# A four-byte touch read ahead of the gate weights: 32 runs instead of 64

## The chip, the cores and the metric

The kernel runs on one core of a Trainium2 chip. The metric is the device time of one execution in microseconds (us), taken over several executions. All executions are fast (no lowered clock, and none over 1.5% above the fastest of its kernel). The profile's span (first to last instruction) is 1.7 to 1.8 us shorter than the device time. The engines are PE (matmul), PEld (its weight load), DVE (vector), ACT (scalar), POOL, and SP, which issues most of the DMAs; ACT issues a few DMAs too.

## The reference

A layer norm of x (2048 x 512) feeds two branches whose outputs are added to x: a state-space layer (a complex linear recurrence over 2048 steps) and a gated feed-forward layer.

```python
xn = layernorm(x)
g = silu(xn @ w_gate)          # w_gate: 512 x 1376
u = xn @ w_up                  # w_up:   512 x 1376
out = x + S5(xn) + (g * u) @ w_down
```

The contraction of 512 is cut into four K tiles of 128 rows.

## The kernel before

The order of the instructions on each engine is computed at build time by a list scheduler from estimated durations; a DMA's estimate contains its byte count. The kernel begins with a start-up in which the first four tiles of x (128 tokens each) are loaded one by one, normalized, transposed on PE, and multiplied with the gate weights as soon as each is there. The loads of this start-up are issued from two queues, SP and ACT, in this order in the code:

```python
x_load(0)                                    # SP, 128 KB
x_load(1)                                    # SP
act_q = [dma("ld_touch", tch[0:16], wg_v[0:128:8, :, 0:2], [("tch",)], 16 * 16, eng="act")]
act_q.append(wg_load("a0", 0, 2, eng="act", order=(act_q[-1],)))   # gate K tiles 0 and 1, 448 KB
x_load(2)                                    # SP
act_q.append(wg_load("a1", 2, 3, eng="act", order=(act_q[-1],)))   # gate K tile 2, 224 KB
wg_load("a2", 3, 4)                          # SP, gate K tile 3
x_load(3)                                    # SP
```

The touch copies two bf16 numbers (4 bytes) from every eighth row of each K tile of the gate weights into a small tile `tch`. No instruction reads `tch`. ACT must issue the touch before it issues the gate load `a0`.

PE fills the time until the first tile is normalized with warm-up matmuls on constants:

```python
pe_warm(9, 512, wbank)
pe_warm(2, 128, wbank)
ln_chunk0()                                  # statistics and normalization of x tiles 0..3 (DVE, ACT)
xt_tile_fine(0, 0, wbank)                    # transposes on PE, evacuated by ACT
# ... (cut) ...
# gate matmuls of one x tile, K tile by K tile: wait for the gate load of that K tile
g.add("pe", mm, reads=[("wg", "a%d" % max(k - 1, 0)) for k in range(k0, k1)] + [("xnTq", q, k) for k in range(k0, k1)], ...)
```

## Time and profile before

The first timing of the kernel was 179.23 us (median of 3).

| What | Value | Where it is read |
|---|---|---|
| PE busy | 173.5 of 177.5 us | page, busy times |
| chain of waits | 96% PE | page, chain |
| x tile 0 landed | 3.10 us | chain |
| first gate matmul | 5.83 us | timeline of PE |
| gate K tiles 0-1 landed | 5.03 us | landings in the trace |

The busy line of the page (busy us, share of the span, instructions; a few matmul records can be missing from a trace):

```profile
PE 173.5 (98%) x935; PEld 83.7 (47%) x935; DVE 162.7 (92%) x284; ACT 88.0 (50%) x116; POOL 11.7 (7%) x22
```

The chain of work that ended last, first 8 us (columns: start us, us, what):

```profile
0.79 2.31 DMA x_sb<-in_A_x_dram
3.10 0.02 issue
3.12 0.71 DVE st L530
...
4.92 0.61 ACT xn_sb L548
5.53 0.05 issue
5.58 0.28 PE pb L582 x2
5.86 0.11 PE pb L477
5.97 1.02 PE pb L803 x18
```

All waits of PE in the whole execution (who waited for whom: us in total, times, longest):

```profile
PE pb L477 <- PEq L1076: 0.8, 1, 0.8
PE pb L582 <- DVE xn_sb L517: 0.6, 1, 0.6
PE pb L582 <- ACT xn_sb L548: 0.2, 1, 0.2
```

The chain begins with a DMA, the load of x tile 0, goes through the normalization on DVE and ACT, and from 5.58 us on it is PE until the last output. And PE waits for nothing after that.

### The profile page before, as it was taken

The page shows a single profiled execution, that of the slowest core. Times are in us where ns is not written, and L with a number is a line of the kernel's source. Part 1 is how long each engine was busy: PE and PEld are TensorE (multiplying, and loading weights), DVE is VectorE, ACT ScalarE, POOL GpSimd, SP SyncE. Part 2 cuts the span into 40 slices and gives each one's busy share as a digit, 9 for nine tenths or more (in the row PEclk, how much of TensorE's full clock was granted, in tenths as well). Part 3 has the DMA queues.
Part 4 walks back from the last instruction along what each step waited for, and adds up shares of the span by engine and source line. Part 5 has one row for each costly group of instructions (what it writes and reads, how often), then busy time and mean ns, then how long its engine had stood idle before and what let it go on. Part 6 is the DMA issues. An engine that isn't in the chain of part 4 may idle for free.

```text
span 177.5 us, 2429 instructions
## 1 busy us (share of the span) xinstructions
PE 173.5 (98%) x935; PEld 83.7 (47%) x935; DVE 162.7 (92%) x284; ACT 88.0 (50%) x116; POOL 11.7 (7%) x22
## 2 busy tenths in 40 slices
PE   7899999999999999999999999999999999999994
PEld 3794444444444444444444444444444444444743
DVE  2966999699999999999999999999999999999933
ACT  4679989679999655026565560000965520000000
POOL 3023300040000000260000000000000000000000
PEclk9999999999999999999999999999999999999999
DMA  5994562664946000001520000001000000001022
GB/s 168 311 365 112 118 131 53 170 145 107 352 100 48 0 0 0 0 30 63 110 39 0 0 0 4 0 30 59 30 0 4 0 0 0 0 0 51 11 89 89
DMA packets 23014, 12.37 MB, mean 70 GB/s; under 512 B 15228, under 2 KB 23004, under 8 KB 23004
## 3 DMA queue, kind: packets, MB, share of 16 engines
q1 hardware_dynamic: 22508, 11.54, 24.7%
q10 hardware_dynamic: 496, 0.69, 1.2%
q8 instruction: 7, 0.11, 0.2%
q14 instruction: 3, 0.02, 0.0%
HBM read 6.46 MB, written 2.10 MB: 48 GB/s over the span
## 4 chain that ended last, share of the span: by engine, by line
PE 96%; DMA 1%; DVE 1%; ACT 1%; issue 0%
PE pb L759 36%; PE pb L959 21%; PE pb L972 16%; PE pb L876 16%; PE pb L803 4%; PE pb L839 2%; DMA x_sb<-in_A_x_dram 1%; PE pb L849 1%; PE pb L582 1%; DVE st L530 0%; ACT xn_sb L548 0%; ACT nm L545 0%; ACT sd L524 0%; DVE x_sb L977 0%; DVE mv L522 0%
## 5 line engine op out<-in xcount | busy, mean ns | idle before, releaser
L916 DVE TENSOR_TENSOR_SCAN rot<-sm,car,rot 128x512 bf16<-128x512 f32 x32 | 38.9, 1266 | 0.1
L959 PE MATMUL pb<-wd,hT 128*128 128x512 bf16 (+3 forms) x198 | 38.8, 355 | 0.0
L759 PE MATMUL pb<-xnT,wu 128*128 128x512 bf16 x160 | 37.3, 379 | 0.0
L759 PE MATMUL pb<-xnT,wg 128*128 128x512 bf16 x132 | 31.3, 379 | 0.0
L972 PE MATMUL pb<-W,hss 128*128 128x512 bf16 (+2 forms) x144 | 28.3, 355 | 0.0
L876 PE MATMUL pb<-xnT,BT 128*128 128x512 bf16 x128 | 28.1, 379 | 0.0
L959 PEld LDWEIGHTS pb<-wd,hT 128*128 128x128 bf16 (+1 forms) x198 | 18.5, 98 | 19.9
L759 PEld LDWEIGHTS pb<-xnT,wu 128*128 128x128 bf16 x160 | 15.6, 98 | 18.9 <-issue 0.2
L829 ACT ACTIVATE uf<-pb 128x1024 bf16<-128x1024 f32 x20 | 20.6, 1028 | 7.3 <-PE pb L759 6.1
L771 ACT ACTIVATE sg<-pb 128x1024 bf16<-128x1024 f32 x20 | 20.2, 1025 | 8.0 <-PE pb L759 7.1
L972 PEld LDWEIGHTS pb<-W,hss 128*128 128x128 bf16 x144 | 13.4, 98 | 14.3
L759 PEld LDWEIGHTS pb<-xnT,wg 128*128 128x128 bf16 x132 | 12.7, 98 | 15.7 <-ACT xn_sb L506 0.4
L876 PEld LDWEIGHTS pb<-xnT,BT 128*128 128x128 bf16 x128 | 12.5, 98 | 15.1
L883 ACT ACTIVATE u_sb<-pb 128x1024 bf16<-128x1024 f32 x16 | 16.2, 1019 | 5.7 <-PE pb L876 5.4
L977 DVE TENSOR_TENSOR x_sb<-pb,x_sb 128x512 bf16<-128x512 f32 (+2 forms) x18 | 11.0, 622 | 3.5 <-PE pb L972 3.4
L831 DVE TENSOR_TENSOR hT<-sg,uf 128x1024 bf16<-128x1024 bf16 x20 | 13.4, 681 | 0.0
L506 ACT ACTIVATE xn_sb<-x_sb,nmr,rstd 128x512 bf16<-128x512 bf16 x8 | 6.0, 803 | 9.6 <-DVE nmr L503 9.6
L858 ACT ACTIVATE sg<-pb 96x1024 bf16<-96x1024 f32 x2 | 2.0, 1014 | 17.1 <-PE pb L839 17.1
L482 DVE BATCH_NORM_STATS2 st<-x_sb 128x6 f32<-128x512 bf16 x12 | 7.4, 682 | 3.2 <-DMA x_sb<-in_A_x_dram 3.2
L907 DVE TENSOR_TENSOR rot<-rot,cosT 128x2048 bf16<-128x2048 bf16 x8 | 9.7, 1218 | 0.1
L907 DVE TENSOR_TENSOR rot<-rot,sin 128x2048 bf16<-128x2048 bf16 x8 | 9.8, 1219 | 0.0
L907 DVE TENSOR_TENSOR rot<-u_sb,cosT 128x2048 bf16<-128x2048 bf16 x8 | 9.7, 1218 | 0.0
(81 smaller groups left out, 145.6 us busy)
## 6 DMA issues: line engine op xcount, KB each, us to landing
out_dram<-x_sb SPq DMA_DIRECT2D x15, 128.0 KB, 1.7
x_sb<-in_A_x_dram SPq DMA_DIRECT2D x3, 512.0 KB, 7.4
wd<-in_B_w_down_dram SPq DMA_DIRECT2D x1, 1280.0 KB, 6.9
wu<-in_B_w_up_dram SPq DMA_DIRECT2D x1, 768.0 KB, 5.3
wu<-in_B_w_up_dram SPq DMA_DIRECT2D x1, 608.0 KB, 7.4
x_sb<-in_A_x_dram SPq DMA_DIRECT2D x4, 128.0 KB, 3.6
wg<-in_B_w_gate_dram SPq DMA_DIRECT2D x1, 480.0 KB, 6.2
wg<-in_B_w_gate_dram ACTq DMA_DIRECT2D x1, 448.0 KB, 3.8
```

The costliest lines, as they stand in the source:

```text
L482: return g.add("dve", lambda e, a=a: e.bn_stats(out=st[:, a, :], in_=x_sb[:, a, :]), reads=[("x", a)], writes=[("st", a)], name="bnst%d" % ...
L759: inst = e.matmul(pbank[0:fs, bk, :].rearrange("p (j t) -> p j t", j=4), lhsT=w[:, kt, i * 128:i * 128 + fs], rhs=xnT[:, c % 2, :, kt, :], ...
L771: g.add("act", lambda e: e.activation(out=sg[rows, sl, 0:n, :].rearrange("p a t -> p (a t)"), in_=pair_f32(rows, bk, 512 * n), func=AF.Sil ...
L829: g.add("act", lambda e: e.activation(out=uf[rows, ul, 0:n, :].rearrange("p a t -> p (a t)"), in_=pair_f32(rows, bk, 512 * n), func=AF.Ide ...
L831: g.add("dve", lambda e: e.tensor_tensor(out=hT[rows, hb, i0:i0 + n, :], in0=sg[rows, sl, 0:n, :], in1=uf[rows, ul, 0:n, :], op=ALU.mult), ...
L876: inst = e.matmul(pbank[:, bk, :].rearrange("p (j t) -> p j t", j=4), lhsT=BT[:, ri, kt, pt * 128:(pt + 1) * 128], rhs=xnT[:, c % 2, :, kt ...
L883: g.add("act", lambda e: e.activation(out=u_sb[:, us].rearrange("p r t -> p (r t)"), in_=pair_f32(slice(0, 128), b0), func=AF.Identity), r ...
L907: tt = lambda out, a, b, op, r, w, nm: g.add("dve", lambda e: e.tensor_tensor(out=out, in0=a, in1=b, op=op), reads=r, writes=w, name="%s_% ...
L916: g.add("dve", lambda e, A0=A0, A1=A1, k=k, ri=ri, pt=pt: e.tensor_tensor_scan(out=A1[:, k, ri, :], data0=rr[:, pt:pt + 1].to_broadcast([1 ...
L959: inst = e.matmul(pbank[:, bk, 0:nc_], lhsT=hT[0:fs, hb, i, lt * 128:(lt + 1) * 128], rhs=wd[0:fs, i, c0:c0 + nc_], start=(i == 0), stop=F ...
L972: inst = e.matmul(pbank[:, bk, 0:nc_], lhsT=hss[:, hb, pt, ri, lt * 128:(lt + 1) * 128], rhs=W12[:, ri, pt, c0:c0 + nc_], start=False, sto ...
L977: g.add("dve", lambda e, bk=bk, a=a, c0=c0, nc_=nc_: e.tensor_tensor(out=x_sb[:, a, c0:c0 + nc_], in0=pbank[:, bk, 0:nc_], in1=x_sb[:, a, ...
```

## The change

The touch was presumably there to reach into the gate weights before the large loads do. The change lets it cover two of the four K tiles, with half as many descriptors. The large loads and everything after them are untouched.

```diff
-        act_q = [dma("ld_touch", tch[0:16], wg_v[0:128:8, :, 0:2], [("tch",)], 16 * 16, eng="act")]
+        act_q = [dma("ld_touch", tch[0:16, 0:2], wg_v[0:128:8, 0:2, 0:2], [("tch",)], 16 * 8, eng="act")]
```

## The prediction

> **What bounds the kernel.** The share table has PE busy 98% of the 177.5 us span (173.5 us). The chain of waits is PE 96%: from the first gate matmul at 5.8 us to 175.2 us it is PE work. PE's waits sum to 1.6 us, all before 5.8 us, none on a weight load. So only the landing of x tile 0 (the chain begins with that DMA, 0.79 to 3.10 us, then DVE and ACT until 5.53 us) or a new gap in PE's stream can move the time.
>
> **What the change does.** The touch read is the first DMA on the ACT queue. Nothing reads its tile or waits for it. It is 64 runs of 4 bytes (16 partitions x 4 K tiles) and becomes 32. The DMA packet records show 4-byte packets of the ACT queue from 1.95 to 2.55 us: 80 of them, 9 ns each. The Trainium skill (DMA: Bandwidth & Descriptors, "Why a DMA increments its semaphore by 16 and not by 1") says that one descriptor moves one contiguous run and that each of 16 engines ends with a semaphore write; 64 + 16 fits. After it I expect 48, or 3 instead of 5 per engine: 18 ns of each engine saved.
>
> **What moves.** The gate load of K tiles 0-1 follows on the same ring: issued at 1.23, first packet at 2.59 us. x tile 0 needed 1.03 us from issue to first packet, so the load could start at about 2.3 to 2.4 us; half of the hold-up, 0.05 to 0.15 us, may be gained. x tile 2 (first packet about 4.0 us, when that load ends) may move as much.
>
> **On the critical path.** Nearly nothing: gate tiles 0-1 at 5.03 us, first used at 5.83 (0.8 slack); tile 2 at 6.09, used at about 6.63 (0.5); tile 3 at 6.59, used at about 7.2 (0.6). x tile 2 lands at 5.91 and DVE reads it at 5.93, but the transposes that this feeds find PE busy. The slack would also cover 0.2 to 0.4 us of slower starts of the two untouched K tiles. Exposed is only x tile 0: its reads end by about 2.53 us, just before the gate load starts. If that load starts 0.1 us earlier, its 1792-byte packets (74 ns and more) meet the tail of x tile 0 or its writes: +0.0 to +0.1 us. Fewer touch packets: -0.02 us.
>
> **Predicted time: 179.2 us**, 8 in 10 between 179.0 and 179.5. Chances: faster by over 2% 0.005, within 2% 0.985, slower by over 2% 0.01.
>
> **What would show it.** 48 packets of 4 bytes on the ACT queue before the first gate load; first 1792-byte packet at about 2.5 us; landing of x tile 0 within 0.1 us of 3.10; first gate matmul within 0.15 us of 5.83; PE waits still without a weight DMA; PE busy within 0.3 us of 173.5.
>
> **What would make it wrong.** (1) The instruction order is computed from estimates that contain the byte count of the touch (256 to 128 bytes, about 1 ns in the model); a near tie could flip an order and cost or save up to 1 us. (2) The touch does more than I think for K tiles 2 and 3, and their loads land over 0.5 us later: PE would wait at about 6.6 or 7.2 us. (3) x tile 0 is delayed by the earlier gate load by more than 0.2 us.

## More of the kernel before

The DMA queue of ACT (packets, MB, share of 16 engines' span) and the touch itself (KB, us from issue to landing):

```profile
q10 hardware_dynamic: 496, 0.69, 1.2%
tch<-in_B_w_gate_dram ACTq DMA_DIRECT2D x1, 0.2 KB, 2.1
```

## The result, and the profile after

The changed kernel took 179.53 us (median of 6, 179.08 to 179.96), the kernel before in the same comparison 179.26 us (179.17 to 179.78). The ratio is 1.0005 with a 95% interval of 0.9983 to 1.0028. (A ratio is the mean time of one kernel's fast runs over that of the other's of the same rounds, so it is not quite the ratio of the medians.) The computed instruction order of every engine is the same as before, apart from the touch.

The same lines of the changed kernel: busy times, then the first part of the chain, then the waits of PE, then the queue of ACT and the touch.

```profile
PE 173.4 (98%) x927; PEld 83.8 (47%) x935; DVE 162.7 (92%) x284; ACT 87.7 (49%) x116; POOL 11.7 (7%) x22
```

```profile
0.79 2.26 DMA x_sb<-in_A_x_dram
...
4.87 0.61 ACT xn_sb L548
5.48 0.05 issue
5.53 0.29 PE pb L582 x2
5.81 0.11 PE pb L477
5.92 1.02 PE pb L803 x18
```

```profile
PE pb L477 <- PEq L1076: 0.8, 1, 0.8
PE pb L582 <- DVE xn_sb L517: 0.2, 1, 0.2
PE pb L582 <- ACT xn_sb L548: 0.2, 1, 0.2
```

```profile
q10 hardware_dynamic: 464, 0.69, 1.1%
tch<-in_B_w_gate_dram ACTq DMA_DIRECT2D x1, 0.1 KB, 2.1
```

The queue of ACT carries 496 - 464 = 32 packets less, exactly the 32 runs taken away. x tile 0 landed 0.05 us earlier (0.79 + 2.26 = 3.05 us), and the gate matmuls began 0.05 us earlier. Nothing else of note happened in this execution. What is left to explain is why nothing happened, what the touch is good for, and where a scatter of 0.9 us comes from.

### The profile page after: what moved, and what is told of

Its sections match the earlier page's. It is cut to its first block, busy times and chain, and to the rows that moved or that the text cites. A ratio compares the mean times of both kernels' runs of the same rounds, so it can differ in the third digit from the quotient of the medians.

```text
span 177.4 us, 2421 instructions
## 1 busy us (share of the span) xinstructions
PE 173.4 (98%) x927; PEld 83.8 (47%) x935; DVE 162.7 (92%) x284; ACT 87.7 (49%) x116; POOL 11.7 (7%) x22
## 4 chain that ended last, share of the span: by engine, by line
PE 95%; DMA 1%; DVE 1%; ACT 1%; issue 0%
PE pb L759 36%; PE pb L959 21%; PE pb L876 16%; PE pb L972 15%; PE pb L803 4%; PE pb L839 2%; DMA x_sb<-in_A_x_dram 1%; PE pb L849 1%; PE pb L582 1%; DVE st L530 0%; ACT xn_sb L548 0%; ACT nm L545 0%; ACT sd L524 0%; DVE x_sb L977 0%; DVE mv L522 0%
## 5 line engine op out<-in xcount | busy, mean ns | idle before, releaser
L959 PE MATMUL pb<-wd,hT 128*128 128x512 bf16 (+3 forms) x194 | 38.1, 355 | 0.2
L759 PE MATMUL pb<-xnT,wu 128*128 128x512 bf16 x160 | 37.3, 379 | 0.0
L759 PE MATMUL pb<-xnT,wg 128*128 128x512 bf16 x132 | 31.3, 380 | 0.0
L759 PEld LDWEIGHTS pb<-xnT,wu 128*128 128x128 bf16 x160 | 15.7, 98 | 18.9 <-issue 0.2
L759 PEld LDWEIGHTS pb<-xnT,wg 128*128 128x128 bf16 x132 | 12.7, 98 | 15.7 <-issue 0.4
```

What stands on the lines that cost most here:

```text
L759: inst = e.matmul(pbank[0:fs, bk, :].rearrange("p (j t) -> p j t", j=4), lhsT=w[:, kt, i * 128:i * 128 + fs], rhs=xnT[:, c % 2, :, kt, :], ...
L959: inst = e.matmul(pbank[:, bk, 0:nc_], lhsT=hT[0:fs, hb, i, lt * 128:(lt + 1) * 128], rhs=wd[0:fs, i, c0:c0 + nc_], start=(i == 0), stop=F ...
```

## The experiments

All were timed with five rounds against the kernel before on the same chip. The first four shared one chip, the next four a second one and the last three a third one. The order of all other instructions was kept as in the changed kernel, except in the last experiment. All results were correct. The edits are shown shortened and against the changed kernel, that of e11 against e2. Two theories stood at the start:

- **Inert**: neither the number of runs nor what they touch matters.
- **Warming**: the touch makes the first real reads of the gate weights quicker, so the half left out is missed.

A third: **spacer**. ACT needs about 0.4 us to issue the touch; that alone keeps the large gate load out of the way while x tile 0 is read.

This table is worked out from the traces of all executions that were profiled, one per kernel and run. A landing is the last of the completion updates of a DMA. "Gate" is the first gate matmul, "full" the first full-width matmul (512 columns) after the start-up (L759), "tail" the time from the start of that to the end of the last DVE add.

```
run           touch runs   x0    x1    K0-1    K2    x2    K3    gate   full   tail
before        64           3.10  4.35  5.03   6.09  5.91  6.59  5.83   12.94  162.57
after         32           3.05  4.07  5.21   6.16  5.81  6.77  5.78   12.86  162.56
e1 (after)    32           2.92  4.77  6.26   6.97  6.60  7.54  6.30   13.64  162.56
e2            none         3.31  4.96  4.63   5.64  5.96  6.56  6.06   13.14  162.57
e3            32, w_up     2.91  3.99  4.97   5.98  5.34  6.55  5.64   12.71  162.57
e4            512          3.07  3.90  5.77   6.75  6.15  6.95  5.82   13.19  162.56
e5            1            2.83  4.38  5.21   6.12  5.55  6.72  5.71   12.92  162.57
e6 (after)    32           3.02  4.00  4.92   6.17  5.49  6.77  5.75   12.83  162.56
e7            32 + 32      3.00  3.46  5.95   7.17  5.29  6.81  6.01   13.46  162.56
e8            32 + 32 + 32 3.72  4.42  5.55   7.29  6.42  7.50  6.45   13.65  162.56
e9            none (swap)  3.84  3.65  5.49   6.17  4.16  6.75  6.72   15.44  162.56
e10           32           2.93  3.98  4.29/5.26  7.24  5.04  7.05  5.98   13.52  162.73
e11           none         3.41  5.00  4.65   5.66  6.00  6.58  6.16   13.24  162.56
```

The last column decides where to look. From the first full-width matmul to the end, twelve of thirteen executions took the same 162.56 or 162.57 us. (In e10 a further 0.17 us went at about 25 us, at the start of the state-space matmuls.) So nearly every difference between these kernels, and between two executions of one kernel, arises in the first 13 us.

### The changed kernel again (e1 and e6)

No edit.

> The changed kernel once more, five rounds, to tell a true difference from the scatter of the first timing (179.08 to 179.96 us). Inert theory (the number of touch runs does not matter): ratio to before within 0.9985 to 1.0015, first packet of the first gate load again near 2.6 us and x tile 0 landing within 0.1 us of 3.1. Rival (the second half of the touch was worth something): ratio 1.001 to 1.002 and clear of 1, with the loads of K tiles 2 and 3 landing later than 6.09 and 6.59 us again.

> The changed kernel a third time. Eleven timings of it so far scatter from 179.08 to 179.98 us, and the profile of its slowest one shows PE waiting 0.3 us for the first gate load, of which one of 16 parts landed 0.85 us after the others. If the change makes such late parts likelier: at least two of five timings above 179.6 us, and the mean 0.1 to 0.25 us above that of before. If it was luck: mean within 0.1 us of before.

e1: ratio 1.0013 (0.9997 to 1.0029), timings 179.12 to 179.98 us. e6: ratio 0.9989 (0.9973 to 1.0005), 179.12 to 179.76 us. In the second comparison it was the kernel before that scattered up to 180.00 us. Together with the first result, 18 timings of the changed kernel have a mean of 179.45 us and the 28 of the kernel before in those comparisons 179.41 us; the difference, 0.04 us, is below its standard error of 0.09 us. The hint of a loss in e1 was by this luck of that comparison. Neither expectation fitted to the letter: in e1 x tile 0 landed at 2.92 us, further from 3.1 us than the 0.1 us that the inert theory allowed, and the mean of e6 lies 0.22 us below that of the kernel before, not within 0.1 us.

The profiled execution of e1 happened to be its slowest, 179.98 us. Its waits of PE, then its chain up to the first gate matmuls:

```profile
PE pb L477 <- PEq L1076: 0.8, 1, 0.8
PE pb L803 <- DMA wg<-in_B_w_gate_dram: 0.3, 1, 0.3
```

```profile
0.79 0.41 ACTq L402
1.20 0.03 issue
1.23 5.03 DMA wg<-in_B_w_gate_dram
6.26 0.04 issue
6.30 1.29 PE pb L803 x18
```

Here the chain begins on ACT's DMA queue and not with x tile 0: x tile 0 landed early (2.92 us), but the gate load of K tiles 0-1 landed at 6.26 us. Of its 16 completion updates, 14 came by 4.96, the fifteenth at 5.41 and the last at 6.26 us: one of sixteen parts was 0.85 us late, and each of the next four loads (K2, x2, K3 and x tile 3) again had a last completion 0.7 us behind its last but one. The slack of 0.8 us that a typical trace shows is real, but a late part uses it up. Why that part was late the trace does not tell. Whether the other slow timings have the same cause was not seen, as only one execution of each run is profiled. A second, smaller source shows in the traces of e1 and e5: the first three gate matmuls start 83 to 107 ns apart and the next ones 55 to 57 ns, which costs about 0.13 us.

### No touch (e2)

```diff
-        act_q = [dma("ld_touch", ...)]
-        act_q.append(wg_load("a0", 0, 2, eng="act", order=(act_q[-1],)))
+        act_q = []
+        act_q.append(wg_load("a0", 0, 2, eng="act")); act_q[0].est += 330.14; act_q[0].nbytes += 54450
```

The last two additions change only the estimates, so that the computed order stays as it was.

> No touch at all; the order of all other instructions is kept (the estimate of the first gate load is raised by what the touch had). Inert theory: time within 0.1 us of before. Spacer theory (the touch matters only because its issue holds the gate load back by 0.4 us, so that x tile 0 reads alone): the first gate packet at 1.9 to 2.2 us instead of 2.6, x tile 0 lands 0.15 to 0.5 us later than 3.1 and the time rises by the same 0.15 to 0.5 us. Warming theory (the touch makes the first reads of the gate weights quicker): first gate packets take longer than now and the first gate load needs clearly more time from its first packet to landing (2.4 us now).

Median 179.55 us (179.45 to 179.73), ratio 1.0012 (1.0000 to 1.0024). The whole of its range lies above the median of the kernel before, 179.25 us. The start of its chain:

```profile
0.79 2.52 DMA x_sb<-in_A_x_dram
3.31 0.02 issue
3.34 0.70 DVE st L530
```

x tile 0 landed at 3.31 us, the gate matmuls began at 6.06 instead of 5.83 us, and the time rose by 0.3 us. So the touch is not inert as a whole: without it the kernel is slower, as the spacer theory expected (this interval alone just reaches 1.0000; e11 repeats it). One of its numbers missed: the gate load was expected to start at 1.9 to 2.2 us and started at 2.65 us. Against the warming theory, the gate load took 1.98 us from its first packet to landing, not more than the 2.43 us of the kernel before. The DMA packet records tell more (counted from the trace: reads of x on SP's queue that had begun by 2.4 us, the last of the 16 completion packets that end x tile 0, the first packet of the first gate load, and the packets of both that began between 3.0 and 3.7 us; in e9, described below, ACT's queue carries x tiles 1 and 2 and has 43 and 124 reads more in the two columns):

```
run      x reads by 2.4   last completion packet of x0   first gate packet   3.0-3.7: x reads   gate packets
before   113              2.60                           2.59                13                  98
after    104              2.65                           2.61                49                  93
e2        44              2.97                           2.65                 0                 150
e11       58              3.05                           2.55                 2                 151
e9        17              3.31                           2.95                13                  71
```

Without the touch, x tile 0 and the gate load are issued at the same moment (0.79 us). The reads of x tile 0 then go at less than half the pace although the gate load's own packets do not begin before 2.65 us. The trace shows where the pace is lost: 12 of the 128 packets of x tile 0 took 406 to 675 ns (in e11 10 of them took 404 to 601 ns), all begun by 2.25 us, where a usual one takes 46 ns; with a touch none of the 128 took over 361 ns in any trace. And x tile 1, issued at 1.25 us, has no packet at all between 3.0 and 3.7 us while the gate load runs: it lands at 4.96 instead of 4.35 us, behind the gate load. In this stretch what was issued first was served first, across the two queues. (If the DMA engines took whole loads from the two queues in turn, it would look the same: both give the order x0, K0-1, x1, K2, x2 that is seen here, and no run tells the two apart.)

### The touch on another tensor (e3)

```diff
-wg_v[0:128:8, 0:2, 0:2]
+wu_v[0:128:8, 0:2, 0:2]
```

> The same 32-run touch, but of the up weights, which the first gate loads do not read. Spacer theory and inert theory: the same time as the changed kernel within 0.1 us, gate loads landing as in it (5.2, 6.2, 6.8 us, each within 0.2). Warming theory: as without a touch, gate landings later by 0.2 us or more.

Median 179.27 us (179.03 to 179.48), ratio 0.9999 (0.9986 to 1.0012). A touch of the up weights, which the first gate loads do not read, does everything that the touch of the gate weights does, and the gate loads land as early (4.97, 5.98, 6.55 us; 0.22 to 0.25 us before the 5.2, 6.2 and 6.8 us expected, a little more than the 0.2 us allowed, but earlier and not later). The reverse can be read too: the up weights were touched here, yet among the first 64 packets of their large load at about 6.3 us, 12 took over 200 ns and the slowest 953 ns, where they had 19 and 674 ns in the kernel before, in which nothing had touched them. The warming theory falls.

### Eight times the runs (e4)

```diff
-tch = sb("tch", [16, KT, 2], B16)
+tch = sb("tch", [128, KT, 2], B16)
-        act_q = [dma("ld_touch", tch[0:16, 0:2], wg_v[0:128:8, 0:2, 0:2], ...
+        act_q = [dma("ld_touch", tch[:], wg_v[:, :, 0:2], ...
```

> The touch eight times the original (128 partitions x 4 K tiles, 512 runs of 4 bytes, 33 packets per engine). If a run costs only its 9 ns of engine time: the first gate load begins 0.2 to 0.3 us later, lands by 5.4 us, before its first use at 5.83; x tile 0 unchanged within 0.1 us; time within 0.15 us of before. If a run costs what the original touch took in sum (0.6 us for 5 packets per engine, 0.12 us each): the first gate load begins about 3 us later, PE waits for it for over 1 us, and the time rises by over 1 us.

Median 179.75 us (179.50 to 179.89), ratio 1.0021 (1.0009 to 1.0033). The first branch of the expectation came nearer: the first gate packet came at 2.90 us, 0.3 us later than with 64 runs (2.59 us), about what 9 ns times 28 more packets per engine gives (0.25 us); x tile 0 was in time (3.07 us). The match may be partly chance: the touch's own packets began later (2.36 instead of 1.95 us) and took no longer from first to last (0.53 against 0.61 us). Its landing and its verdict on the time were wrong, though. The gate loads landed at 5.77 (not by 5.4) and 6.75 us, and in the chain PE stops for K tile 2:

```profile
5.94 0.83 PE pb L803 x14
6.77 0.11 issue
6.88 0.38 PE pb L803 x4
```

After 14 matmuls (two K tiles of seven) PE needs K tile 2, which landed at 6.75 us. The slack behind the gate loads is therefore small: this kernel is 0.4 us slower (means: 179.70 against 179.31 us for the kernel before; the profiled execution, 179.53 us, shows 0.25 us of it at the first full-width matmul). From 64 to 32 runs the same arithmetic gives 2 packets per engine, or 18 ns, which no comparison here can see.

### One run of four bytes (e5)

```diff
-tch[0:16, 0:2], wg_v[0:128:8, 0:2, 0:2]
+tch[0:1, 0:1], wg_v[0:1, 0:1, 0:2]
```

> A touch of a single run of 4 bytes: the issue on ACT stays (0.4 us), the descriptors go from 32 to 1. Spacer theory (only the place of the first gate load in the order of issue counts, behind x tile 1): first gate packet at 2.45 to 2.65 us as with 32 and 64 runs, x tile 1 lands by 4.4 us, before the gate load is done, time 179.2 to 179.4 us. Descriptor theory (the runs themselves hold the gate load back): as without a touch, first x reads slow, x tile 1 landing near 4.9 us, time 179.5 us or more.

Median 179.21 us (179.15 to 179.48), ratio 0.9986 (0.9972 to 1.0000). The queue of ACT confirms that next to nothing of the touch is left (464 - 418 = 46 packets less than the changed kernel: 31 runs and 15 completions):

```profile
q10 hardware_dynamic: 418, 0.69, 1.1%
```

x tile 0 landed at 2.83 us and the time was as good as with 32 or 64 runs. The issue of the touch on ACT suffices; its data do not matter. The first gate packet, at 2.73 us, was slightly later than expected; the issue of this touch took 0.52 instead of 0.41 us, so the gate load was issued at 1.34 instead of 1.23 us.

### Two touches (e7), and everything later (e8)

```diff
 act_q = [dma("ld_touch", tch[0:16, 0:2], ...)]
+act_q.append(dma("ld_touch2", tch[0:16, 2:4], wg_v[0:128:8, 2:4, 0:2], ..., eng="act"))    # e7 and e8
+dma("ld_touch3", tch[0:16, 4:6], wg_v[0:128:8, 2:4, 0:2], ...)                             # e8 only: SP, ahead of x_load(0)
```

(In e8 `tch` is made twice as wide. The estimates of the added DMAs are set to 0, so that the order of the rest stays.)

> The original 64 runs in two DMAs of 32 on ACT, so that the first gate load is issued 0.4 us later (1.65 instead of 1.23 us) and comes behind x tile 2 in the order of issue. Spacer theory: x tile 1 and x tile 2 land earlier (x tile 2 by about 5.2 instead of 5.9 us), the first gate load later by 0.3 to 0.5 us (5.3 to 5.5 us, first use at 5.8), the time within 0.2 us of before or up to 0.4 us longer when a late part of it passes 5.8 us. Inert theory: all landings as before.

> One more touch of 32 runs ahead of x tile 0 on SP and one more on ACT, so that all first loads are issued 0.4 us later in the same order. If the chain begins with x tile 0 and nothing after it has slack, as the prediction says: x tile 0 lands near 3.5 us and the time rises by 0.35 to 0.45 us, ratio 1.002 to 1.0025. If there is slack behind x tile 0: less than 0.2 us.

e7: median 179.65 us, ratio 1.0005 (0.9991 to 1.0020) against a kernel before that scattered widely; its mean, 179.61 us, is 0.32 us above that of e6 on the same chip (179.28 us). As expected x tiles 1 and 2 landed earlier (3.46 and 5.29 us) and the gate loads later (5.95 and 7.17 us), later even than the 0.3 to 0.5 us foreseen. PE waited for K tile 2:

```profile
PE pb L803 <- DMA wg<-in_B_w_gate_dram: 0.3, 1, 0.3
```

There is a second cost that had not been foreseen: ACT issues DMAs and computes. Its table load begins after the last issue. It began at 2.23 us before and at 2.70 us in e7, and the square root that the normalization needs came at 4.20 us although x tile 0 was earlier (3.00 us). Timeline of ACT in e7 (start us, us, what):

```profile
1.71 0.96 ACTq L402 DMA_DIRECT2D wg<-in_B_w_gate_dram  x2
2.70 1.28 ACT L466 ACT_TABLE_LOAD   x1 [2.70 <-issue]
4.00 0.29 ACT L466 ACTIVATE sm<-epst 128x1 f32<-128x1 f32 x1
4.20 0.28 ACT L524 ACTIVATE sd<-mv,epst 128x1 f32<-128x1 f32 x1
```

Before, the same two activations stood at 3.52 and 4.07 us with a wait of 0.25 us between them. One spacer fits in front of the table load, a second does not. In this trace that cost is hidden, as the chain runs through K tile 2 (landed at 7.17 us).

e8: median 179.82 us, ratio 1.0021 (1.0007 to 1.0035), as expected for a delay of 0.4 us that passes to the end. In its profile x tile 0 was issued at 1.25 us and landed at 3.72 us, later than the 3.5 us expected:

```profile
0.79 0.39 SPq L402
1.18 0.07 issue
1.25 2.47 DMA x_sb<-in_A_x_dram
3.72 0.02 issue
```

Compared with the profiled execution of e6, x tile 0 came 0.70 us later, the gate matmuls 0.70 us later (6.45 against 5.75 us) and the full-width matmuls 0.82 us later. There is no slack behind x tile 0.

### Another spacer (e9)

After the order has been computed, x tiles 1 and 2 are moved to ACT, the gate loads to SP behind x tile 0, and the touch is dropped:

```diff
+for e_, ns in (("act", ["ld_x1", "ld_x2"]), ("sp", ["ld_x0", "ld_wga0", "ld_wga1", "ld_wga2"])):
+    streams[e_] = [dl[n] for n in ns] + [t for t in streams[e_] if t.name not in early]
```

> No touch, but the same order of issue as with it: x tiles 1 and 2 go out on ACT, x tile 0 and the gate loads on SP, so that the first gate load is the second DMA of SP (issued at about 1.2 us) behind x tile 0 and x tile 1; the order of every other instruction is kept. Spacer theory: any DMA that holds the first gate load in its place does what the touch does: gate loads and x tiles 1 and 2 land within 0.25 us of their places in the changed kernel, time within 0.15 us of it. Rival (x tile 0 lands late whenever a large load is issued at the same moment, 0.79 us, as the run without a touch suggests): x tile 0 at 3.2 us or later and the time 0.15 to 0.35 us longer. If the touch does something of its own: also longer, with x tile 0 in time.

Median 179.80 us (179.60 to 181.78), ratio 1.0022 (1.0008 to 1.0036). The rival was right about x tile 0: x tile 0 and x tile 1, both issued at 0.79 us, landed together at 3.84 and 3.65 us, and by 2.4 us only 17 reads of x tile 0 had begun. (By the ratio the time rose by 0.39 us, a little more than the 0.35 us it allowed.) The chain:

```profile
0.79 3.05 DMA x_sb<-in_A_x_dram
3.84 0.02 issue
3.86 0.70 DVE st L530
```

So the late landing in e2 was no peculiarity of the gate weights: another large load issued at the same moment, x tile 1, goes with a late x tile 0 too. The three kernels with a late x tile 0 (e2, e9, e11) are, however, also the three without a touch, and no run has a touch and another large load both issued at 0.79 us; that the touch itself does something is thus not excluded by them. x tile 1 speaks against it: in the kernels with a touch it is issued within 0.1 us of the first gate load and lands 2.65 to 3.52 us after its issue, but in e7, where the second touch is issued beside it in place of the gate load, 2.21 us after. The order of issue was not kept as intended either, as x tile 2 (1.21 us) came ahead of the gate load (1.25 us) and landed at 4.16 us. The profiled execution, 181.78 us, had bad luck on top, which the other five timings (up to 180.04 us) do not show: PE waited 0.7 us before the first transposes and ran the first gate matmuls at half the pace. Timeline of PE (start us, us, what), e9:

```profile
6.72 2.13 PE L803 MATMUL pb<-xnT,wg 128*128 128x128 bf16 x18
```

The same 18 matmuls took 1.16 us in the changed kernel. From the first of them to the transposes behind them it is 1.92 us in e9 and 1.00 us in the changed kernel, or 107 and 56 ns for each. The Trainium skill ("TensorE: Matmul & The Clock Gate", section "What you observe") gives these very two gaps, 107 and 56 ns, for a PE before and after its warm-up. The trace agrees: its record of the clock grants PE the full clock only from 10.23 us on, where the kernel before had it from 3.52 us.

### The first gate load in two (e10)

```diff
-wg_load("a0", 0, 2, ...)                    # K tiles 0 and 1
+wg_load(K tile 0), wg_load(K tile 1)        # two DMAs on ACT; the first seven gate matmuls wait for K tile 0 alone
```

> The touch as changed; the first gate load in two, K tile 0 and K tile 1, so that the first seven gate matmuls wait for K tile 0 alone. If the scatter of the timings above 179.3 us comes from late parts of the first gate load, its worst timing falls by up to 0.4 us and the mean by about 0.1 us below that of before. If it comes from x tile 0 or from the loads of K tiles 2 and 3, the mean is that of before within 0.1 us, or up to 0.3 us worse, as the later gate loads are issued 0.45 us later.

Median 179.87 us (179.58 to 180.07), ratio 1.0029 (1.0016 to 1.0041): worse, by 0.5 us, more than the 0.3 us that was expected at most. K tile 0 landed at 4.29 us, far ahead of its use, but the third issue on ACT pushed the table load to 2.68 us as in e7 and K tile 2 to 7.24 us. PE waited for it:

```profile
PE pb L803 <- DMA wg<-in_B_w_gate_dram: 0.4, 1, 0.4
```

This was an attempt at a version better than both. It failed, and it leaves open how much of the scatter comes from late parts of the first gate load, as a new wait replaced the one that it was to remove.

### No touch, with the order that the scheduler computes (e11)

```diff
-act_q.append(wg_load("a0", 0, 2, eng="act")); act_q[0].est += 330.14; act_q[0].nbytes += 54450
+act_q.append(wg_load("a0", 0, 2, eng="act"))
```

> No touch, as in the second experiment, but without the correction of the estimates, so that the computed order of DVE changes in two places (a near tie, risk 1 of the prediction). Expected from the second experiment: x tile 0 lands at 3.2 us or later and the time is 179.4 to 179.75 us. If the order of DVE matters: the stretch from the first full-width gate matmul to the last DVE add, 162.57 us in all ten profiles so far, changes by over 0.1 us. If it does not: 162.5 to 162.6 us again. If x tile 0 lands by 3.1 us this time, the late landing of the second experiment was luck.

Median 179.55 us (179.39 to 179.62), ratio 1.0012 (0.9999 to 1.0024), x tile 0 at 3.41 us: the second experiment once more. Together, the ten timings without a touch have a mean of 179.54 us and the 20 of the kernel before 179.30 us: 0.24 us, about five times its standard error of 0.05 us. Two places of DVE's order differ, and the tail is 162.56 us as everywhere. The late landing without a touch came in both traces without one and in none of the nine in which x tile 0 is issued first beside a single touch or ahead of everything else (2.83 to 3.10 us).

No kernel tried here is clearly faster than the kernel before. The touch with a single run is as good as the larger ones; its interval reaches 1.0000.

## Why the prediction was right or wrong, point by point

- **Time: right in substance, the range too narrow.** 179.2 us and no change were predicted. By the ratio the changed kernel takes 1.0005 x 179.26 = 179.35 us, and the mean of all 18 timings is 179.45 us; both lie in the range of 179.0 to 179.5. The median of the first six, 179.53 us, lies just above it. The range was read off three timings within 0.12 us; single executions scatter over 0.9 us.
- **The bound: right.** The chain begins with x tile 0 and is PE from 5.6 us on; e8 showed that a delay of x tile 0 passes to the end, and twelve of thirteen profiles have the same 162.56 or 162.57 us from the first full-width matmul on. That the start-up could also end with a gate load was ruled out too firmly: in e1, with the same kernel, it did. And in e5, where x tile 0 landed earliest (2.83 us), the chain begins with PE's own warm-up matmuls (0.83 to 5.04 us), so a still earlier x tile 0 would not have helped there.
- **Cost of the runs: right.** 32 packets less, 9 ns each, 18 ns per engine. e4 fits it from the other side (28 more packets per engine than before, and 0.3 us), but does not prove it, as its touch also began 0.41 us later.
- **The step that failed: "half of the hold-up, 0.05 to 0.15 us, may be gained", with the first gate packet at about 2.5 us.** It was at 2.61 us, where it had been at 2.59 us. The estimate had taken the wait of the gate load for a wait behind the touch. The runs do not bear that out: with 64, 32 or 1 run the load starts between 2.45 and 2.75 us (2.73 us with 1 run), and without any touch, issued 0.44 us earlier, still at 2.65 and 2.55 us. In two other traces of the changed kernel, e1 and e6, it did start at 2.45 us, as predicted; but the five traces with 32 runs have a mean of 2.57 us and a spread of 0.3 us, so that no gain can be told. Only 512 runs hold it back (2.90 us). In before, after, e1 and e3 its first packet lies within 0.1 us of the last completion packet of x tile 0, as if it waited for the data ahead of it, but in e5, e6 and e10 it is 0.2 to 0.3 us away, so this is a reading and no proof. So halving the touch gained nothing there that these traces can show, nor did it endanger x tile 0; what the load does wait for stays open. The shifts of x tile 1, x tile 2 and the gate loads between the two profiles (up to 0.28 us) are smaller than those between two profiles of the changed kernel itself (e1 and e6: 0.77 us for x tile 1).
- **"PE waits still without a weight DMA": half right.** True in two of three profiles of the changed kernel. In the third PE waited 0.3 us for the first gate load. The slack of 0.8 us was read from one execution, and a transfer in 16 parts is only as early as its last part.
- **Risk 1, a changed order: did not happen.** The order is the same with 256 and 128 bytes. Where it did change (e11), the tail kept its length.
- **Risk 2, the untouched K tiles: refuted** by e3: the touch warms nothing.
- **Risk 3, x tile 0 delayed by the gate load: the right danger with the wrong trigger.** It came true when the two were issued at the same moment (e2, e11), not when the touch was made shorter.

Two statements of the Trainium skill carried the argument. "DMA: Bandwidth & Descriptors", section "Why a DMA increments its semaphore by 16 and not by 1", says that one descriptor moves one contiguous run and that only the engines in use post a completion while the issuing sequencer writes the rest at once. The packet counts of the ACT queue agree to the packet: 496, 464, 418 and 944 for 64, 32, 1 and 512 runs, and for the single run the semaphore changed at 1.39 us and then at 1.97 us. The section "Issuing engines are not separate DMA queues" of the same page says that DMAs from all engines run on the same 16 DMA engines, and that issuing on several engines saves only the issue time. The runs agree with the first half: a load issued on ACT delays one issued on SP. They show beside it that the issue time may be just what is wanted: with 0.4 us of it between them, x tile 0 landed by 3.10 us, without it at 3.31 and 3.41 us.

What stays open: why the first packets of x tile 0 are so long in e2 and e11, and its pace about half or less (44 and 58 reads by 2.4 us against 113), while the other load has no packets yet; and why single parts of a load come up to 0.85 us late. The number of runs issued beside x tile 0 is not the reason for the first: in e4 it was 512, twice that of the gate load in e2, and x tile 0 landed at 3.07 us.

## What to carry to other kernels

A tiny DMA whose result nobody reads can matter through the time that its issue takes: before resizing it, ask whether its bytes or its place in the order of issue do the work, and test it with a single descriptor and with none at all. Try issuing the load at the head of the critical chain alone: here a lead of 0.4 us over the next large one was worth 0.24 us, and no other lead was tried. And slack read from one trace is that of one execution: look at all 16 completions and at a second trace before you spend it.

## What the Trainium skill lacked or had wrong

- "DMA: Bandwidth & Descriptors", section "Queues, rings and completion order", says that each DMA engine goes round-robin between the queues that have work and drains a whole packet, typically of about 9 to 17 descriptors, from one before it switches. The runs do not contradict it: the first gate load has 256 runs and 16 completions, 17 for each of 16 engines, and without a touch x tile 1 (issued at 1.25 us on SP) had no read between 3.0 and 3.7 us while that load (issued at 0.79 us on ACT) had 150. What the page lacks is whether the order of issue counts as well; no run here tells.
- The same page lacks that a load can be slow from its start when another large one is issued at the same moment: 44, 58 and 17 reads of x tile 0 begun by 2.4 us in the three kernels with such a pair at 0.79 us, against 97 to 137 in the nine traces in which it is issued first beside a single touch or ahead of everything else, and a landing 0.2 to 0.7 us later than before.
- The same page lacks the spread of the completions of one DMA: in one execution 14 of 16 were there by 4.96 us and the last at 6.26 us.
- The same page, section "Issuing engines are not separate DMA queues", calls the issue time usually small relative to the DMA itself. Here it was 0.41 us on ACT for a touch of 256 bytes, and on an engine that computes it also delayed its table load, from 2.23 to 2.70 us for one issue more.
